# A gated feed-forward kernel on one core: its last store is made by two queues, half of the partitions each

## The chip, the cores and the metric

The kernel runs on one core of a Trainium2 chip. The metric is device time in microseconds: how long one execution takes. The core has a matrix engine (TensorE, PE in the profile), VectorE (DVE), ScalarE (ACT), GpSimd (POOL) and SyncE (SP). Transfers between device memory and the core's memory are started by an engine's queue and carried by 16 DMA engines.

## The reference

```python
B, S, D, F = 32, 32, 1024, 3584        # x: (B, S, D); w_gate, w_up: (D, F); w_down: (F, D); all bf16
def reference(x, w_gate, w_up, w_down):
    return (_gelu(x @ w_gate) * (x @ w_up)) @ w_down      # _gelu: the tanh approximation
```

With the batch flattened, x has N = 1024 rows. The result is 1024 x 1024 in bf16.

## The kernel before

There are two phases of matmuls. In the first, chunks of 128 columns of F (28 of them) are multiplied for 256 or 512 rows of x at a time: eight matmuls for the gate and eight for the up product, ScalarE applies the gelu (line 444), and VectorE multiplies the two and leaves the product in `hT` (line 484). In the second phase (lines 411 to 428) the output is made in jobs: a job is one block of 128 rows (`tc`) and a stretch of columns, and takes 28 matmuls that add up in one bank of PSUM. Sixteen jobs of 512 columns would cover the output; the last of them is cut into one of 384 and one of 128 columns, so there are NJ = 17. The last job, number 16, is the one of 128 columns.

Every engine runs its own program, and waits on counters (semaphores). The program of each engine is written as a function: `prog_sp`, `prog_act`, `prog_pool`, `prog_pe`, `prog_dve`. A `_Clock` is one semaphore with the count that it will have reached; `do` issues an instruction and adds to a clock, and `wait` (line 41 emits it) holds an engine until a clock has reached a value. DMA clocks go up by 16 for each transfer.

The results of jobs leave PSUM in turns: even jobs by ScalarE (line 450), odd jobs by VectorE (line 490), both into `osb`, which is the same memory as `xT` and appears under that name in the profile. After each eviction SyncE stores the job's columns to the output, one DMA for a job, all on SyncE's own queue and on the clock `Q_OUT` (line 343). After the last one it waits for `Q_OUT` to reach its total, and with that the kernel ends. So the last steps in order are: last matmul of job 16 on TensorE, eviction of 128 x 128 by ScalarE, store of 128 partitions x 256 bytes (32 KB) by SyncE, and SyncE's wait for its landing.

ScalarE also has a DMA queue, which it uses for a part of x at the start (lines 296 and 287); it issues no transfer after that.

Of the kernel before, what the change touches and what calls it, by code (L numbers as in the profile page):

```python
# [5 lines left out]
P = 128  # L6
# [78 lines left out]
def bass_standalone__geglu_ffn__sampling_kernel(  # L85
# [120 lines left out]
    jobs.append((ltc, lcol + lnc - P, P, 0 if lbank != 0 else 2))  # L206
    NJ = len(jobs)

    def evac_eng_is_act(ji):
        return ji % 2 == 0  # L210

    out_r = of.rearrange("(tc p) d -> p tc d", p=P)
# [7 lines left out]
    C_ACT = _Clock("act")  # L220
# [7 lines left out]
    Q_WD_SP = _Clock("wd_sp", 16)  # L228
    Q_WD_POOL = _Clock("wd_pool", 16)
    Q_OUT = _Clock("out", 16)  # L230
    all_clocks = [C_PE, C_ACT, C_DVE, C_POOL, *Q_XA, *Q_X.values(), *Q_W0.values(), *Q_WG, *Q_WU,
                  Q_WD_SP, Q_WD_POOL, Q_OUT]

    ctx = _Ctx()

    with ExitStack() as es:
# [18 lines left out]
        osb = xT  # L255
# [14 lines left out]
        def issue_wd(ew, eng, mine, upto_chunk, clock, force=False):  # L270
            for k in list(mine):
                if force or wd_gate_chunk[k] <= upto_chunk:
                    ew.wait(C_PE, ctx.get(("U", last_part[wd_gate_chunk[k]])))
                    a, b = wd_groups[k]
                    ew.do(lambda: eng.dma_start(wd[:, a:b, :], wd_r[:, a:b, :]), clock=clock)  # L275
                    mine.remove(k)

        def load_w(ew, eng, w, j):
            c0, gsz, buf = groups[j]
            q = (Q_WG if w == "wg" else Q_WU)[j]  # L280
            ctx.set((w, j), ew.do(lambda: eng.dma_start(  # L281
                wbuf(w, buf)[:, :, 0:gsz * P], w_r[w][:, :, c0 * P:(c0 + gsz) * P]), clock=q))
# [12 lines left out]
        def early_loads(ew, eng, side):  # L295
            ctx.set(("xa", side), ew.do(lambda: eng.dma_start(  # L296
                xa[:, side, :], xa_r[:, side, :]), clock=Q_XA[side]))
            yield
            if side == 0:
                for k in range(DK):  # L300
                    for w in ("wg", "wu"):
                        load_w0(ew, eng, w, k)
            ew.wait(Q_W0[("wu", 5)], ctx.get(("wu0", 5)))
            for q in XPIECES:
                load_x(ew, eng, q, side)

        def gate_w(ew, j):
            if war[j] is None:
                for s in range(2):
                    ew.wait(Q_X[(XC2, s)], ctx.get(("x", XC2, s)))  # L310
                return -1
            ew.wait(C_PE, ctx.get(("U", last_part[war[j]])))
            return war[j]
# [15 lines left out]
        def prog_sp(eng):  # L329
            sp = _Eng(ctx, eng, None)  # L330
            for _ in early_loads(sp, eng, 0):
                pass
            wd_mine = [k for k in range(len(wd_groups)) if k % 2 == 0]
            for j in range(NG):
                known_chunk = gate_w(sp, j)
                load_w(sp, eng, "wg", j)
                issue_wd(sp, eng, wd_mine, known_chunk, Q_WD_SP)
            issue_wd(sp, eng, wd_mine, FM, Q_WD_SP, force=True)
            ctx.set("wd_sp_total", Q_WD_SP.n)
            last = None  # L340
            for ji, (tc, col0, ncols, b) in enumerate(jobs):
                sp.wait(C_ACT if evac_eng_is_act(ji) else C_DVE, ctx.get(("E", ji)))
                last = sp.do(lambda: eng.dma_start(
                    out_r[:, tc, col0:col0 + ncols],
                    osb[:, tc, col0:col0 + ncols]), clock=Q_OUT)
            sp.wait(Q_OUT, last)

        def turn_xa(pe, eng, b, dk):
            pe.wait(Q_XA[b], ctx.get(("xa", b)))
            j, (bank, k0, k1, b0, b1) = next(  # L350
                (j, c) for j, c in enumerate(XA_PS) if c[1] <= dk < c[2] and c[3] <= b < c[4])
            o = P * ((b1 - b0) * (dk - k0) + b - b0)
            last = dk == k1 - 1 and b == b1 - 1
            v = pe.do(lambda: eng.matmul(  # L354
                ps[:, bank, o:o + P],
                xa[:, b, :].rearrange("p (j k) -> p j k", k=DK)[:, :, dk],
                ident[:, :], start=(dk == k0 and b == b0), stop=last), mark=last)
            if last:
                ctx.set(("XP", j), v)
# [36 lines left out]
        def prog_pe(eng):  # L396
# [14 lines left out]
            for ji, (tc, col0, ncols, b) in enumerate(jobs):  # L411
                if b in bank_last_job:
                    pj = bank_last_job[b]
                    pe.wait(C_ACT if evac_eng_is_act(pj) else C_DVE, ctx.get(("E", pj)))
                else:
                    pe.wait(C_DVE, ctx.get(("D", owner[b])))
                bank_last_job[b] = ji
                v = None
                for m in range(FM):
                    pe.wait(C_DVE, ctx.get(("D", last_part[m])))  # L420
                    last = (m == FM - 1)
                    v = pe.do(lambda: eng.matmul(  # L422
                        ps[:, b, 0:ncols],
                        hT[:, m, tc * P:(tc + 1) * P],
                        wd[:, m, col0:col0 + ncols],
                        start=(m == 0), stop=(m == FM - 1),
                    ), mark=last)
                ctx.set(("O", ji), v)

        def prog_act(eng):  # L430
            act = _Eng(ctx, eng, C_ACT)
            act.do(lambda: eng.activation(warm[:, 0:1], const0, ACTF.Gelu_apprx_tanh))
            for _ in early_loads(act, eng, 1):
                for j, (bank, k0, k1, b0, b1) in enumerate(XA_PS):
                    act.wait(C_PE, ctx.get(("XP", j)))
                    nt = P * (b1 - b0)
                    ctx.set(("XA", j), act.do(lambda: eng.activation(  # L437
                        xT[:, k0:k1, P * b0:P * b1],
                        ps[:, bank, 0:nt * (k1 - k0)].rearrange("p (k t) -> p k t", t=nt), ACTF.Copy)))
            for i, (m, t0, t1, (gb, g0, g1), us) in enumerate(parts):  # L440
                act.wait(C_PE, ctx.get(("U" if us[0] == gb else "G", i)))
                if i >= NTB:
                    act.wait(C_DVE, ctx.get(("D", i - NTB)))
                ctx.set(("A", i), act.do(lambda: eng.activation(  # L444
                    t_bufs[i % NTB][:, 0:t1 - t0], ps[:, gb, g0:g1], ACTF.Gelu_apprx_tanh)))
            for ji, (tc, col0, ncols, b) in enumerate(jobs):
                if not evac_eng_is_act(ji):
                    continue
                act.wait(C_PE, ctx.get(("O", ji)))
                ctx.set(("E", ji), act.do(lambda: eng.activation(  # L450
                    osb[:, tc, col0:col0 + ncols], ps[:, b, 0:ncols], ACTF.Copy)))

        def prog_dve(eng):
            dve = _Eng(ctx, eng, C_DVE)
# [37 lines left out]

        progs = [
            (prog_sp, nc.sync, "sync"),
            (prog_act, nc.scalar, "scalar"),
            (prog_pool, nc.gpsimd, "gpsimd"),
            (prog_pe, nc.tensor, "tensor"),
# [44 lines left out]
```

## Time and profile before

| what | us |
|---|---|
| median of 3 runs | 299.48 (299.15 to 299.63) |
| the profiled execution, its time | 298.94 |
| the profiled execution, its span | 297.6 |
| TensorE busy in the span | 293.6 |
| VectorE, ScalarE, GpSimd busy | 64.3, 42.4, 7.9 |
| last eviction by ScalarE: start, length | 295.85, 0.28 |
| last store's issue by SyncE: start, length | 296.15, 0.33 |
| last store, from issue to landing | 1.4 |
| SyncE's last wait, for that landing | 1.1 |

The span is what the profile sees of the program; the execution's time holds a little more than it. All times inside the profile count from the span's start. SPq, ACTq and PEq are the queues of instructions of SyncE, ScalarE and TensorE, and DMA_DIRECT2D is the instruction that issues a transfer; its length is the time of the issue alone, and the bytes move afterwards. Times of landing count from the issue.

### The profile page before, as it was taken

The numbers are of one execution on the slowest core, as the hardware profiler recorded it, in microseconds if no ns is written. First come the engines' busy times: TensorE is split into PE (matmuls) and PEld (weight loads), VectorE is DVE, ScalarE is ACT, GpSimd is POOL, SyncE is SP. The second block draws the span as 40 slices with busy tenths as digits, with TensorE's granted clock in tenths as the row PEclk, the third lists the DMA queues.
The fourth block names the chain that finished last, engine by engine and source line by source line (L and its number), as shares of the span: only waits on it lengthen the run. The fifth ranks groups of instructions, "written<-read, shape, count | busy, mean of one in ns | idle before, by whom it ended". The sixth has DMA issues, their size and how long they took to land.

```text
span 297.6 us, 3491 instructions
## 1 busy us (share of the span) xinstructions
PE 293.6 (99%) x1528; PEld 147.9 (50%) x1552; DVE 64.3 (22%) x108; ACT 42.4 (14%) x79; POOL 7.9 (3%) x14
## 2 busy tenths in 40 slices
PE   8999999999999999999999999999999999999997
PEld 5899644444444444444444444444444444444445
DVE  4669721111121111122111122110000000000000
ACT  4032211221111121111121111110000000000000
POOL 1001001020000002001000000000000000000000
DMA  7988004766009301942104000000000100010001
GB/s 263 391 194 263 23 2 147 276 203 224 0 0 305 120 0 38 373 156 100 43 0 141 0 2 0 0 0 20 18 18 20 35 18 18 20 35 18 18 20 35
DMA packets 17806, 26.43 MB, mean 89 GB/s; under 512 B 1152, under 2 KB 11392, under 8 KB 17792
## 3 DMA queue, kind: packets, MB, share of 16 engines
q1 hardware_dynamic: 13840, 16.78, 17.2%
q0 software_dynamic: 2176, 8.39, 7.8%
q10 hardware_dynamic: 1776, 1.05, 1.4%
q8 instruction: 12, 0.20, 0.3%
q14 instruction: 2, 0.02, 0.0%
HBM read 24.12 MB, written 2.10 MB: 88 GB/s over the span
## 4 chain that ended last, share of the span: by engine, by line
PE 97%; DMA 1%; issue 0%; SPq 0%; ACT 0%
PE ps L385 65%; PE ps L422 32%; DMA wgbig<-in_w_gate_dram 1%; SPq L296 0%; ACT xT L450 0%
## 5 line engine op out<-in xcount | busy, mean ns | idle before, releaser
L422 PE MATMUL ps<-wd,hT 128*128 128x512 bf16 (+2 forms) x468 | 96.5, 366 | 0.4
L385 PE MATMUL ps<-xT,wubig 128*128 128x512 bf16 (+2 forms) x395 | 79.5, 336 | 0.3
L385 PE MATMUL ps<-xT,wgbig 128*128 128x512 bf16 (+2 forms) x394 | 79.2, 336 | 0.4
L422 PEld LDWEIGHTS ps<-wd,hT 128*128 128x128 bf16 x476 | 45.5, 98 | 51.6
L484 DVE TENSOR_TENSOR hT<-tb,ps 128x512 bf16<-128x512 f32 (+1 forms) x64 | 38.9, 613 | 131.6 <-PE ps L385 131.6
L444 ACT ACTIVATE tb<-ps 128x512 f32<-128x512 f32 (+1 forms) x64 | 34.3, 544 | 158.0 <-PE ps L385 157.5
L385 PEld LDWEIGHTS ps<-xT,wgbig 128*128 128x128 bf16 x400 | 38.1, 98 | 31.8 <-DVE xT L475 0.3
L385 PEld LDWEIGHTS ps<-xT,wubig 128*128 128x128 bf16 x400 | 38.1, 98 | 31.5 <-DMA wubig<-in_w_up_dram 0.2
L385 PE MATMUL ps<-xT,wgsmall 128*128 128x512 bf16 x126 | 30.1, 379 | 0.1
L385 PE MATMUL ps<-xT,wusmall 128*128 128x512 bf16 x125 | 29.8, 379 | 0.2
L490 DVE CAST xT<-ps 128x512 bf16<-128x512 f32 (+1 forms) x8 | 5.4, 675 | 89.6 <-PE ps L422 89.6
L385 PEld LDWEIGHTS ps<-xT,wgsmall 128*128 128x128 bf16 x128 | 12.5, 98 | 15.1
L385 PEld LDWEIGHTS ps<-xT,wusmall 128*128 128x128 bf16 x128 | 12.5, 98 | 15.1
L450 ACT ACTIVATE xT<-ps 128x512 bf16<-128x512 f32 (+1 forms) x9 | 5.1, 562 | 93.1 <-PE ps L422 93.1
L475 DVE STREAM_TRANSPOSE xT<-hT 128x128 bf16<-128x128 bf16 (+2 forms) x20 | 13.5, 708 | 4.7 <-DMA hT<-in_x_dram 4.7
L460 DVE STREAM_TRANSPOSE xT<-hT 32x192 bf16<-32x192 bf16 x16 | 8.2, 515 | 4.6 <-DMA hT<-in_x_dram 4.2
L281 POOL DMA_DIRECT2D wubig<-in_w_up_dram x3 | 2.7, 886 | 63.1 <-PE ps L385 63.1
L399 PE MATMUL ps<-const-bfloat16-1.0 128*128 128x512 bf16 (+1 forms) x10 | 3.0, 476 | 0.8 <-PEq L527 0.8
L281 POOL DMA_DIRECT2D wusmall<-in_w_up_dram x2 | 2.0, 994 | 47.1 <-PE ps L385 26.0
L275 POOL DMA_DIRECT2D wd<-in_w_down_dram x3 | 2.3, 768 | 19.1 <-PE ps L385 19.1
L399 PEld LDWEIGHTS ps<-const-bfloat16-1.0 128*128 128x128 bf16 x10 | 1.2, 134 | 2.4 <-issue 2.4
L437 ACT ACTIVATE xT<-ps 128x128 bf16<-128x128 f32 (+1 forms) x4 | 1.5, 437 | 1.9 <-PE ps L354 1.9
(10 smaller groups left out, 4.5 us busy)
## 6 DMA issues: line engine op xcount, KB each, us to landing
wd<-in_w_down_dram SPq DMA_DIRECT2D x4, 1024.0 KB, 11.4
wgbig<-in_w_gate_dram SPq DMA_DIRECT2D x3, 1024.0 KB, 5.7
wubig<-in_w_up_dram POOLq DMA_DIRECT2D x3, 1024.0 KB, 9.7
wd<-in_w_down_dram POOLq DMA_DIRECT2D x3, 1024.0 KB, 11.4
wgbig<-in_w_gate_dram SPq DMA_DIRECT2D x8, 256.0 KB, 5.4
wubig<-in_w_up_dram SPq DMA_DIRECT2D x8, 256.0 KB, 5.5
wgsmall<-in_w_gate_dram SPq DMA_DIRECT2D x2, 1024.0 KB, 5.9
wusmall<-in_w_up_dram POOLq DMA_DIRECT2D x2, 1024.0 KB, 9.6
```

What stands on the lines that cost most here:

```text
L275: ew.do(lambda: eng.dma_start(wd[:, a:b, :], wd_r[:, a:b, :]), clock=clock)
L281: ctx.set((w, j), ew.do(lambda: eng.dma_start(wbuf(w, buf)[:, :, 0:gsz * P], w_r[w][:, :, c0 * P:(c0 + gsz) * P]), clock=q))
L385: v = pe.do(lambda: eng.matmul(ps[:, bank, f0:f1], wbuf(w, buf)[:, dk, slot * P:(slot + 1) * P], xT[:, dk, t0:t1], start=first, stop=last ...
L399: pe.do(lambda: eng.matmul(ps[:, 0, 0:n], ones_w, ones_x[:, 0:n], start=True, stop=True), mark=False)
L422: v = pe.do(lambda: eng.matmul(ps[:, b, 0:ncols], hT[:, m, tc * P:(tc + 1) * P], wd[:, m, col0:col0 + ncols], start=(m == 0), stop=(m == F ...
L437: ctx.set(("XA", j), act.do(lambda: eng.activation(xT[:, k0:k1, P * b0:P * b1], ps[:, bank, 0:nt * (k1 - k0)].rearrange("p (k t) -> p k t" ...
L444: ctx.set(("A", i), act.do(lambda: eng.activation(t_bufs[i % NTB][:, 0:t1 - t0], ps[:, gb, g0:g1], ACTF.Gelu_apprx_tanh)))
L450: ctx.set(("E", ji), act.do(lambda: eng.activation(osb[:, tc, col0:col0 + ncols], ps[:, b, 0:ncols], ACTF.Copy)))
L460: v = dve.do(lambda: eng.transpose(xT[32 * a:32 * (a + 1), XA_DVE[0]:XA_DVE[1], XA[0]:XA[1]].rearrange("p k (b t) -> p k b t", t=P)[:, :, ...
L475: v = dve.do(lambda: eng.transpose(xT[:, dk, q[0]:q[1]].rearrange("p (c i) -> p c i", i=32), src))
L484: ctx.set(("D", i), dve.do(lambda: eng.tensor_tensor(hT[:, m, t0:t1], t_bufs[i % NTB][:, 0:t1 - t0], ps[:, ub, u0:u1], ALU.mult)))
L490: ctx.set(("E", ji), dve.do(lambda: eng.tensor_copy(osb[:, tc, col0:col0 + ncols], ps[:, b, 0:ncols])))
```

## The change

The last store, of job 16, is split by partitions. SyncE stores partitions 0 to 63 on `Q_OUT`, and ScalarE stores partitions 64 to 127 on its own queue and a new semaphore, `Q_OUT2`, after it has waited for its own eviction to be counted. SyncE at the end waits for both semaphores. The other 16 stores stay as they were. The new assertion states that the last job is one that ScalarE evicts.

```diff
+    assert NJ % 2 == 1
+
     def evac_eng_is_act(ji):
         return ji % 2 == 0
...
     Q_OUT = _Clock("out", 16)
+    Q_OUT2 = _Clock("out2", 16)
...
             for ji, (tc, col0, ncols, b) in enumerate(jobs):
                 sp.wait(C_ACT if evac_eng_is_act(ji) else C_DVE, ctx.get(("E", ji)))
+                p1 = P // 2 if ji == NJ - 1 else P
                 last = sp.do(lambda: eng.dma_start(
-                    out_r[:, tc, col0:col0 + ncols],
-                    osb[:, tc, col0:col0 + ncols]), clock=Q_OUT)
+                    out_r[0:p1, tc, col0:col0 + ncols],
+                    osb[0:p1, tc, col0:col0 + ncols]), clock=Q_OUT)
             sp.wait(Q_OUT, last)
+            sp.wait(Q_OUT2, ctx.get("out2"))
...
                 ctx.set(("E", ji), act.do(lambda: eng.activation(
                     osb[:, tc, col0:col0 + ncols], ps[:, b, 0:ncols], ACTF.Copy)))
+            act.wait(C_ACT, ctx.get(("E", NJ - 1)))
+            ctx.set("out2", act.do(lambda: eng.dma_start(
+                out_r[P // 2:P, tc, col0:col0 + ncols],
+                osb[P // 2:P, tc, col0:col0 + ncols]), clock=Q_OUT2))
```

More of the change, by code (lines that the diff above doesn't have):

```diff
@@ L230, in bass_standalone__geglu_ffn__sampling_kernel @@
     Q_OUT = _Clock("out", 16)
+    Q_OUT2 = _Clock("out2", 16)
     all_clocks = [C_PE, C_ACT, C_DVE, C_POOL, *Q_XA, *Q_X.values(), *Q_W0.values(), *Q_WG, *Q_WU,
-                  Q_WD_SP, Q_WD_POOL, Q_OUT]
+                  Q_WD_SP, Q_WD_POOL, Q_OUT, Q_OUT2]
     ctx = _Ctx()
```

## The prediction

> **What bounds the kernel now.** I read the engine table, then the chain of waits, then the last microseconds as a timeline, in windows and by transfers, because the edit touches only the last store.
>
> The engine table and the summary of the chain:
>
> ```profile
> PE 293.6 (99%) x1528; PEld 147.9 (50%) x1552; DVE 64.3 (22%) x108; ACT 42.4 (14%) x79; POOL 7.9 (3%) x14
> ...
> PE 97%; DMA 1%; issue 0%; SPq 0%; ACT 0%
> ```
>
> TensorE is never short of work, and 97% of the chain is matmuls. Nothing that the edit changes lies in them. The chain written out in time ends like this (start, length, what):
>
> ```profile
> 281.55 14.28 PE ps L422 x93
> 295.82 0.02 issue
> 295.85 0.28 ACT xT L450
> ```
>
> After the last matmul ScalarE evicts the last 128 columns from 295.85 to 296.13. The timeline shows what follows (start, length, engine; SPq is SyncE's queue):
>
> ```profile
> 295.85 0.28 ACT L450 ACTIVATE xT<-ps 128x128 bf16<-128x128 f32 x1 [5.52 <-PE ps L422]
> 296.15 0.33 SPq L343 DMA_DIRECT2D out_dram<-xT  x1
> ```
>
> and three windows split the rest (window, length, busy time of five engines, clock, share of the DMA engines, GB/s):
>
> ```profile
> 296.15:296.95 0.80, 0.00 (x0) 0.00 (x0) 0.00 (x0) 0.00 (x0) 0.00 (x0) 1.00 0.00 0
> 296.95:297.25 0.30, 0.00 (x0) 0.00 (x0) 0.00 (x0) 0.00 (x0) 0.00 (x0) 1.00 0.50 109
> 297.25:297.62 0.37, 0.00 (x0) 0.00 (x0) 0.00 (x0) 0.00 (x0) 0.00 (x0) 1.00 0.00 0
> ```
>
> The tail is thus 1.47 us: 0.80 until the first byte moves (0.33 of it the issue), 0.30 of moving, 0.37 until SyncE sees the completion and stops. No compute engine works in it. Only this tail, 0.5% of the span, is open to the change.
>
> **The reference point.** The profiled execution took 298.94 us: span 297.6 and 1.3 outside it. The median of the runs is 299.48 (299.15 to 299.63), so the profiled one is 0.5 lower. The sum below is a difference in the profiled tail, and I add it to the median. About 0.2%, or 0.6 us, is what a measurement of this kernel can tell from no change; "same" means within that.
>
> **SyncE's half.** It waits for the same eviction and issues at 296.15 as before. The store goes from 128 rows of 256 bytes to 64. Two prices are open. The issue: stores of 128, 96 and 32 KB all took 0.33, so it does not follow bytes, and a load with only 32 partitions (the x pieces, line 287) took 0.33 too, so it does not seem to follow partitions either, though that one still had 128 pieces in all. I take 0.33; if it halved it would give 0.16. The rest, from the list of transfers (size, median us from issue to landing):
>
> ```profile
> out_dram<-xT SPq DMA_DIRECT2D x15, 128.0 KB, 1.7
> ...
> out_dram<-xT SPq DMA_DIRECT2D x1, 96.0 KB, 1.6
> out_dram<-xT SPq DMA_DIRECT2D x1, 32.0 KB, 1.4
> ```
>
> 96 KB less saves 0.3 us, so 16 KB less saves 0.05; if the moving phase halved with the rows it would save 0.15. But the other 16 KB move at the same moment, so the 32 KB of before still have to pass. I take 0 and keep 0.05 and 0.15 as lower bounds, 0.31 with the halved issue.
>
> A rule speaks against the change here. The Trainium skill, in "DMA: Bandwidth & Descriptors", section "Rules for kernel authors", says of two transfers to disjoint partition halves that they share the same 16 DMA engines and serialize, and advises one transfer of 128 partitions. By that rule the saving is the 0 that I took; by halving it would be 0.15. No run here shows the case.
>
> **ScalarE's half.** It is new, and nothing is queued behind it on ScalarE. It is the new end of the chain if it lands after SyncE's. Terms, each relative to SyncE's issue at 296.15:
> - It first waits for ScalarE's own eviction to be counted. The trace has no such wait on ScalarE. The nearest row is SyncE's start 0.02 after the eviction's end, which gives a lateness of 0. GpSimd's wait on its own iota (ends 1.06, next starts 1.15) is 0.09 long, so 0.07 late. GpSimd is a far relative; I take 0.03.
> - Issue on ScalarE is longer. In the pair of x loads at the start SyncE's took 0.38 and ScalarE's 0.40; in the pair at 12.61 they took 0.33 and 0.37. Also, ScalarE has issued nothing since about 16 us. SyncE's first store after an idle stretch of 48 us took 0.37, later ones 0.33. So between 0.02 and 0.08; I take 0.05.
> - ScalarE's queue may start late; that is the first rival below. In the sum it is 0.
>
> **SyncE's second wait.** SyncE now waits for two semaphores in turn. One such wait takes 0.02 (17 ns, SyncE's waits at line 41). The first passes while the second half is still on its way, so it is hidden if ScalarE's half is last, and costs 0.02 if not. I take 0.02.
>
> **The rest.** The list of instructions of the new kernel shows one more DMA on ScalarE, 64x128, after the last eviction, and SyncE's last store cut to 64x128; every other engine has the same list. PE, DVE and GpSimd do nothing in the tail. So: 0 + 0.03 + 0.05 + 0.02 = +0.10 us, that is 299.48 + 0.10 = 299.58, a hair slower and not measurable.
>
> **Rival 1, slower: ScalarE's queue lags.** The only place where both queues start together on quiet DMA engines is the load of x at the start:
>
> ```profile
> 0.73 0.38 SPq L296 DMA_DIRECT2D hT<-in_x_dram  x1
> ...
> 0.79 0.40 ACTq L296 DMA_DIRECT2D hT<-in_x_dram  x1
> ```
>
> ```profile
> hT<-in_x_dram SPq DMA_DIRECT2D x1, 256.0 KB, 2.8
> hT<-in_x_dram ACTq DMA_DIRECT2D x1, 256.0 KB, 3.3
> ```
>
> Counted from its own issue, ScalarE's landed 0.5 later. If that lag belongs to the queue, the end moves by 0.5 and the upper ends of the other terms, 0.07 + 0.08 + 0.02: +0.67, giving 300.15, slower by 0.22%. Against it: those transfers are 256 KB each, which at the 393 GB/s of the window from 2.70 to 3.70 need 0.65 to move, so the second may only have stood behind the first's bytes; 16 KB at 109 GB/s take 0.15. And among the smaller x pieces (64 KB) the medians are 3.8 and 3.9, a lag of 0.1. The rival decides once the lag passes 0.5. Chance 0.20.
>
> **Rival 2, a little slower: one issue at a time.** If ScalarE's issue can't begin before SyncE's 0.33 is over, the end moves by 0.33 + 0.10 = +0.43: 299.91, still within 0.2%. The pair at 12.61 speaks against it: both issues began at 12.61 and took 0.33 and 0.37, so neither stood still for the other's 0.33. Chance 0.10. The Trainium skill has such a rule in "Perfetto Trace Analysis", section "DMA Instruction — HWDGE (DVE, Sync)": the descriptor generator is locked for the exclusive use of one sequencer, and the wait for it lies inside the profiled duration. The trace does not agree, at least at the size of 0.33, in that pair.
>
> **Rival 3, faster: the halves run truly beside each other.** Then both the moving phase and the issue shrink with the rows: 0.15 + 0.16 = 0.31 less, 299.17. To be measurably faster it would have to take 0.6 out of a tail of 1.47, of which 0.37 is completion after the last byte and 0.47 (0.80 less 0.33) passes between the end of the issue and the first byte; together with the issue these fixed parts are nearly all of the 1.4 to which the landing fell from 1.7 when the bytes fell to a quarter. Chance 0.12.
>
> That the change doesn't do what it says can be left out: the two stores of 64 rows stand on the two engines in the list of instructions.
>
> **How the numbers follow.** Forecast 0.58 at 299.58; rival 1 0.20 at 300.15; rival 2 0.10 at 299.91; rival 3 0.12 at 299.17. The runs of before spread by 0.3 downward and 0.15 upward of their median, so a case near a border falls on both sides. Slower by over 0.2% (above 300.08): 0.17 from rival 1, 0.04 from rival 2, 0.03 from the forecast: 0.24. Faster by over 0.2% (below 298.88): 0.07 from rival 3, which also stands for any shrinking of the fixed parts that no row shows, and 0.02 from the forecast: 0.09. The rest, 0.67, is within. The range goes from 299.15, where rival 3 lies, to 300.15, where rival 1 does.
>
> **What would show it.** In the changed kernel's profile ScalarE's store should start at 296.15 to 296.22 on the scale of this span and last 0.35 to 0.41; SyncE's should start 0.02 after the eviction's end and last 0.33; both should land 1.35 to 1.5 after their issue; and SyncE's last wait should be for ScalarE's semaphore. A lag of 0.5 or more between the two landings makes rival 1 right, an issue of 0.65 or more on one of the two makes rival 2 right, and landings of 1.2 or less with a shorter issue make rival 3 right. If the time moves by over 0.6 us while the tail moves by less than 0.3, the cause lies in something that I held to be untouched, and the prediction is wrong in its premise.

## The result, and the profile after

The change makes the kernel slower: 300.10 us median against 299.39 (14 runs each), ratio 1.0024 with a 95% interval of 1.0017 to 1.0032. At 299.39 that is 0.51 to 0.96 us, 0.72 in the middle. The middle lies just beyond the 0.2% that the prediction set as the border of what can be told, the lower end just short of it.

TensorE is again busy for 99% of the span, and the chain (the work that ended last, followed back) is again matmuls; the chain of before began with a load, 1% of it, which the edit does not touch. The 2.0 us more of TensorE are no sign of more work: the profile of before holds only 1528 of the 1552 matmuls.

```profile
PE 295.6 (99%) x1552; PEld 148.6 (50%) x1552; DVE 64.4 (22%) x108; ACT 42.3 (14%) x79; POOL 7.9 (3%) x14
...
PE 99%; ACT 0%; issue 0%
```

This execution's span is 298.8, 1.2 more than the one of before, and half of that has nothing to do with the edit: the last eviction starts at 296.45 instead of 295.85, before any changed instruction runs. Such starts scatter from one profiled execution to the next (296.06 to 297.11 in the experiments), so below only the tail is compared, from the issue of the last store to the end of the span. The timeline of the tail (start, length, engine):

```profile
296.45 0.28 ACT L455 ACTIVATE xT<-ps 128x128 bf16<-128x128 f32 x1 [5.52 <-PE ps L427]
296.75 0.55 SPq L347 DMA_DIRECT2D out_dram<-xT  x1
296.75 0.56 ACTq L458 DMA_DIRECT2D out_dram<-xT  x1
```

Both queues start in the same moment, 0.02 after the eviction, but the issues take 0.55 and 0.56 where SyncE's took 0.33 before. The windows of the tail (window, length, busy time of five engines, clock, share of the DMA engines, GB/s):

```profile
296.75:297.95 1.20, 0.00 (x0) 0.00 (x0) 0.00 (x0) 0.00 (x0) 0.00 (x0) 1.00 0.00 0
297.95:298.20 0.25, 0.00 (x0) 0.00 (x0) 0.00 (x0) 0.00 (x0) 0.00 (x0) 1.00 0.32 66
298.20:298.45 0.25, 0.00 (x0) 0.00 (x0) 0.00 (x0) 0.00 (x0) 0.00 (x0) 1.00 0.33 66
298.45:298.84 0.39, 0.00 (x0) 0.00 (x0) 0.00 (x0) 0.00 (x0) 0.00 (x0) 1.00 0.00 0
```

Nothing moves for 1.20 us (0.80 before). Then there are two moving phases of 0.25, one after the other: by the packets' records the first holds only packets of SyncE's queue, the second only those of ScalarE's. The completion takes 0.39 (0.37 before). The tail is 2.09 against 1.47: +0.62, which lies inside the interval of the timed runs. The transfers (size, us from issue to landing):

```profile
out_dram<-xT SPq DMA_DIRECT2D x1, 16.0 KB, 1.8
out_dram<-xT ACTq DMA_DIRECT2D x1, 16.0 KB, 2.0
```

Half of the bytes take 1.8 to land on the queue that took 1.4 for all of them, and SyncE's last wait lasts 1.5 instead of 1.1.

### The profile page after: what moved, and what is told of

Read it like the earlier page. It is cut to its first block, busy times and chain, and to the rows that moved or that the text cites. A ratio compares the mean times of both kernels' runs of the same rounds, so it can differ in the third digit from the quotient of the medians.

```text
span 298.8 us, 3516 instructions
## 1 busy us (share of the span) xinstructions
PE 295.6 (99%) x1552; PEld 148.6 (50%) x1552; DVE 64.4 (22%) x108; ACT 42.3 (14%) x79; POOL 7.9 (3%) x14
## 4 chain that ended last, share of the span: by engine, by line
PE 99%; ACT 0%; issue 0%
PE ps L390 65%; PE ps L427 32%; PE ps L404 1%; PE ps L359 0%; ACT xT L455 0%
## 5 line engine op out<-in xcount | busy, mean ns | idle before, releaser
L390 PE MATMUL ps<-xT,wgbig 128*128 128x512 bf16 (+2 forms) x400 | 80.5, 339 | 0.0
```

Source lines behind the costliest of these rows:

```text
L390: v = pe.do(lambda: eng.matmul(ps[:, bank, f0:f1], wbuf(w, buf)[:, dk, slot * P:(slot + 1) * P], xT[:, dk, t0:t1], start=first, stop=last ...
```

## The experiments

Three theories were to be told apart: A, two issues in the same moment stretch each other; B, a store of 64 rows is itself slow; C, ScalarE's queue is slow. The tails of all timed kernels, from the records of the trace in us, stand in one table. Each row is one profiled execution; the ratio is of the timed runs. "First byte" counts from the start of the store's own issue, in the order of the issues.

| kernel | issue | first byte | tail | tail less 1.47 | ratio to before (95%) |
|---|---|---|---|---|---|
| before | 0.33 | 0.83 | 1.47 | | |
| the change | 0.55, 0.56 | 1.21, 1.47 | 2.09 | +0.62 | 1.0024 (1.0017 to 1.0032) |
| both halves on SyncE | 0.55, then 0.60 | 1.21, 1.25 | 2.46 | +0.99 | 1.0032 (1.002 to 1.0044) |
| whole on ScalarE | 0.37 | 0.87 | 1.53 | +0.05 | 1.0002 (0.9992 to 1.0012) |
| SyncE's half alone | 0.55 | 1.21 | 1.80 | +0.33 | 1.0009 (0.9997 to 1.0022) |
| ScalarE's half later | 0.55, 0.53 | 1.21, 1.19 | 2.15 | +0.68 | 1.0024 (1.0013 to 1.0035) |
| halves by columns | 0.33, 0.37 | 0.83, 0.91 | 1.64 | +0.17 | 1.0008 (0.9994 to 1.0021) |
| 96 and 32 rows | 0.35, 0.38 | 0.85, 0.93 | 1.68 | +0.20 | 1.0005 (0.9996 to 1.0014) |
| the change, not for the first time | 0.47, 0.51 | 1.13, 1.39 | 2.02 | +0.54 | 1.0012 (0.9998 to 1.0026) |

**Both halves on SyncE.** The second queue is taken away, the cut by partitions stays.

```diff
+            ctx.set("out2", sp.do(lambda: eng.dma_start(
+                out_r[P // 2:P, tc, col0:col0 + ncols],
+                osb[P // 2:P, tc, col0:col0 + ncols]), clock=Q_OUT2))
...
-            act.wait(C_ACT, ctx.get(("E", NJ - 1)))
-            ctx.set("out2", act.do(lambda: eng.dma_start(
...
```

> SyncE issues both halves, one after the other, on its own queue; ScalarE issues none. Theory A (two issues at once stretch each other): no two issues overlap, so each takes 0.33 as before, the first half lands 1.4 after its issue, the second is issued about 0.4 later and lands 1.4 to 1.5 after that: end 0.35 to 0.45 later than before, 0.2 to 0.3 earlier than the change. Theory B (a store of 64 rows is itself slow to issue): both issues take 0.55, the second half lands about 0.6 + 1.8 after the first issue: end 0.8 to 1.0 later than before, later than the change. Theory C (ScalarE's queue is slow): as A, the end 0.35 to 0.45 later than before.

Timeline of its two issues:

```profile
296.37 0.55 SPq L347 DMA_DIRECT2D out_dram<-xT  x1
296.96 0.60 SPq L350 DMA_DIRECT2D out_dram<-xT  x1
```

The first takes 0.55 with no other issue beside it, and the end is 0.99 later. Theory A falls, B holds. The second issue's 0.60 says less: in the probes below, stores of other counts took as long when they came right behind a store of 64 rows. So the second queue saves something against one queue (2.09 against 2.46); the cut itself is what loses.

**Whole on ScalarE.** The cut is taken away, the other queue stays.

```diff
+                if ji == NJ - 1:
+                    continue
...
-                out_r[P // 2:P, tc, col0:col0 + ncols],
...
+                out_r[0:P, tc, col0:col0 + ncols],
...
```

> ScalarE alone issues the last store, whole, 128 rows; SyncE only waits for it. Theory A: no second issue beside it, so ScalarE's issue takes 0.35 to 0.41, landing 1.4 to 1.55, end 0.0 to 0.15 later than before. Theory B: the store has 128 rows, so the same as A. Theory C: issue 0.55 and landing 2.0, end 0.55 to 0.7 later than before, all that the change cost.

```profile
297.42 0.37 ACTq L459 DMA_DIRECT2D out_dram<-xT  x1
```

The issue takes 0.37, the landing 1.5, and the time is that of before. Theory C falls: ScalarE's queue, unused for 280 us, costs about 0.05.

**SyncE's half alone.** Partitions 64 to 127 of the last job are left unstored, and ScalarE issues nothing.

> SyncE stores partitions 0 to 63 of the last job as in the change; partitions 64 to 127 of the last job are not stored at all, and ScalarE issues nothing. Theory A: nothing overlaps, so the issue takes 0.33 or less, landing 1.3 to 1.4, end 0 to 0.15 earlier than before. Theory B: issue 0.55, landing 1.8, end about 0.3 to 0.4 later than before. Theory C: as A.

```profile
296.53 0.55 SPq L347 DMA_DIRECT2D out_dram<-xT  x1
```

Theory B again: with half of the store thrown away and nothing beside it, the issue takes 0.55, the first byte comes at 1.21 and the tail grows by 0.33. The ratio alone (its interval includes 1) would not have shown it; the tail does.

**ScalarE's half later.** ScalarE makes two scratch evictions before it issues.

```diff
-            act.wait(C_ACT, ctx.get(("E", NJ - 1)))
+            for k in range(2):
+                v = act.do(lambda: eng.activation(t_bufs[k][:, 0:P], ps[:, b, 0:P], ACTF.Copy))
+            act.wait(C_ACT, v)
```

> As the change, but ScalarE makes two more evictions of the same 128 columns into scratch (about 0.28 each) before it issues its half, so that its issue begins about 0.6 after SyncE's. Theory A: SyncE's issue is over by then and takes 0.33 again, its half lands 1.4 after the issue; ScalarE's issue takes 0.35 to 0.41 and lands 1.4 to 1.5 after it: end 0.6 to 0.7 later than before, about equal to the change although ScalarE started 0.6 later. Theory B: both issues take 0.55 as in the change, end 1.1 to 1.2 later than before. Theory C: SyncE's issue 0.33, ScalarE's 0.55 and landing 2.0: end 1.1 to 1.2 later.

The two evictions overlapped each other and the one before, so that ScalarE issued 0.34 after SyncE and not 0.6; the expected ends do not apply as written. Still, both issues keep their 0.53 to 0.55 although ScalarE's starts when SyncE's is more than half over. ScalarE's first byte comes 1.19 after its issue instead of 1.47, so that 0.34 of delay at the issue cost only 0.06 at the end. Counted from its own issue, ScalarE's half lands after 1.76 here and after 2.04 in the change, where its first byte comes 0.27 after SyncE's.

**Which counts of rows are slow.** Two probes cut the stores of jobs 1 to 14 (6 us apart) in many ways on SyncE's queue; the edit only changes which rows and columns each store takes, and sends the rest right after the first part of the next job's store. The issues compared here are those of the first parts, which have nothing directly in front of them in the queue.

> A probe of store shapes on SyncE's queue alone. The stores of jobs 1 to 14, about 6 us apart and long landed before the end, are cut: the first part goes out after its eviction, the rest right after the first part of the next job's store. First parts: 64, 96, 32, 16, 112, 64 (the upper ones), 80 and 48 rows of 512 columns; 64 rows of two separate stretches of 128 columns; 128 rows of two such stretches; 32 rows of four stretches of 64; 128 rows of 128 and of 64 columns; 64 rows of 128. The last store is whole, as before. What is asked is the length of each issue. Theory B1 (fewer than 128 rows cost 0.2 us of issue): 0.55 for every first part with fewer than 128 rows, whatever its columns and pieces, 0.33 for 128 rows. Theory B2 (fewer than 128 pieces cost it): 64 rows of two stretches and 32 rows of four are 128 pieces and take 0.33; 64, 96, 32, 16 rows of one stretch take more than 0.33. Theory B3 (only the count of 64 is slow): 0.55 for 64 rows alone, 0.33 for the other counts. Theory A (two at once) says 0.33 throughout, and has lost already for SyncE.

Issues of 64 rows, 32 rows, 64 rows of two separate stretches of columns, 32 rows of four stretches, and 64 rows of 128 columns, in that order, from the timeline of the first probe:

```profile
212.52 0.54 SPq L339 DMA_DIRECT2D out_dram<-xT  x1
224.61 0.32 SPq L339 DMA_DIRECT2D out_dram<-xT  x1
248.78 0.63 SPq L339 DMA_DIRECT2D out_dram<-xT  x1
260.87 0.33 SPq L339 DMA_DIRECT2D out_dram<-xT  x1
278.90 0.47 SPq L339 DMA_DIRECT2D out_dram<-xT  x1
```

16, 48, 80 and 112 rows took 0.32 to 0.34, 96 rows and 128 rows of 128 columns 0.36, the upper 64 rows 0.47. Only the count of 64 is slow (theory B3): not fewer rows, not fewer pieces (64 rows of two stretches are 128 pieces and take 0.63; 32 rows of four are as many and take 0.33), not the bytes. It is slow with 128 and with 512 columns, and dearer at its first use than later.

The rest of each job shows one thing more. A store of a quick count took 0.32 to 0.47 to issue when it was sent right behind another quick one, and 0.58 to 0.61 right behind one of 64 rows, even with 16, 32, 120 or 128 rows. This is the store of 16 rows behind the upper 64:

```profile
243.16 0.58 SPq L339 DMA_DIRECT2D out_dram<-xT  x1
```

> A second probe of store shapes on SyncE's queue, made like the first: the first parts of the stores of jobs 1 to 14 are 32 rows of two separate stretches (64 pieces), 64 rows from the middle (32 to 95), 64, 63, 65, 56, 72, 8 rows, 64 rows of four stretches, 60 rows, 96 rows of two stretches, 64 rows, 120 rows, 32 rows. If the count of 64 rows alone is slow: 0.47 to 0.55 for each part of 64 rows wherever it lies, more with more stretches, and below 0.40 for all others, 32 rows of two stretches too. If 64 pieces are what is slow, 32 rows of two stretches take 0.47 or more. Odd counts (63, 65) or counts that 16 does not divide may spread over fewer DMA engines and take another time; nothing in the case says which.

From the second probe: 32 rows of two stretches, 63 rows, and 65:

```profile
212.38 0.34 SPq L339 DMA_DIRECT2D out_dram<-xT  x1
230.41 0.33 SPq L339 DMA_DIRECT2D out_dram<-xT  x1
236.56 0.31 SPq L339 DMA_DIRECT2D out_dram<-xT  x1
```

64 rows from the middle took 0.62 and 64 rows of four stretches 0.65; 8, 56, 60, 72, 96 (two stretches) and 120 rows took 0.28 to 0.34. The two neighbours of 64 are quick to issue. The store of 63 rows then met something else: 56 of its rows had moved 1.3 us after the issue, but the last seven moved only from 232.13 on, when a 16 KB transfer on the queue of instructions, begun at 230.74, was over; and the store sent right behind it took 1.75 to issue, which no other did. Why 64 is slow, no run shows.

**Pairs.** A probe sends parts of the even jobs from SyncE and ScalarE in the same moment.

> A probe of pairs. At even jobs, about 12 us apart, SyncE and ScalarE each store a part in the same moment, after ScalarE's eviction: 64 + 64 rows of 512 columns; 128 rows, 256 + 256 columns; 128 rows, 64 + 64 columns; 64 + 64 rows of 128 columns (the change's own shape); ScalarE alone a whole 128 x 512; SyncE alone 64 rows; ScalarE alone 64 rows; 64 + 64 rows of two stretches of 128 columns. What is left over goes out later on SyncE; the last store is whole on SyncE, as before. If two issues in the same moment hinder each other only in what comes after the issue: 0.55 on both for pairs of 64 rows, 0.33 and 0.37 for pairs of 128 rows, ScalarE's half landing 0.2 to 0.3 later than SyncE's in each pair, and ScalarE alone landing 1.75 after its issue with 64 rows. If they stretch each other's issue: 0.55 or more on the pairs of 128 rows as well. If ScalarE's queue is slow by itself: its 64 rows alone land 2.0 after the issue.

A pair of 64 + 64 rows, and one of 128 rows cut by columns:

```profile
207.45 0.55 SPq L342 DMA_DIRECT2D out_dram<-xT  x1
207.45 0.56 ACTq L342 DMA_DIRECT2D out_dram<-xT  x1
...
219.53 0.36 SPq L342 DMA_DIRECT2D out_dram<-xT  x1
219.54 0.38 ACTq L342 DMA_DIRECT2D out_dram<-xT  x1
```

ScalarE alone took 0.47 for 64 rows, which landed after 1.93 (SyncE's alone after 1.92), and 0.34 for a whole store: the price of 64 belongs to both queues, and a pair of 128 rows pays nothing of it. ScalarE's first byte was 0.28 behind SyncE's in the first pair, 0.09 in the second, and 0.09 in a later pair of exactly the change's shape (the fourth, with issues of 0.51 and 0.50). The lag is not simply a wait until SyncE's bytes are through: in the first pair they move for 0.45, and ScalarE's begin 0.17 before they end.

**Halves by columns.** The two queues stay, each with 128 rows of 64 columns.

```diff
-                p1 = P // 2 if ji == NJ - 1 else P
+                n1 = ncols // 2 if ji == NJ - 1 else ncols
...
-                out_r[P // 2:P, tc, col0:col0 + ncols],
...
+                out_r[:, tc, col0 + ncols // 2:col0 + ncols],
...
```

> The last store is split between the two queues as in the change, but by columns: SyncE stores 128 rows of the first 64 columns, ScalarE 128 rows of the other 64. If the rows are what cost (theory B): both issues 0.33 to 0.37, first bytes 0.80 after them, ScalarE's half behind SyncE's by 0.1 to 0.3, tail from the end of the eviction 1.6 to 1.8 us: end 0.1 to 0.3 later than before and 0.3 to 0.5 earlier than the change. If two issues at once stretch each other: both 0.55, tail 2.1, as the change.

```profile
296.36 0.33 SPq L347 DMA_DIRECT2D out_dram<-xT  x1
296.37 0.37 ACTq L458 DMA_DIRECT2D out_dram<-xT  x1
```

The same cut in two without the count of 64: issues of before, ScalarE's first byte 0.08 behind SyncE's, tail +0.17. That is what a second queue costs here when the rows are right, and it still gains nothing.

**96 and 32 rows.** One number of the change is altered, `p1 = 96`, with ScalarE's rows from 96 on.

> As the change, but SyncE stores 96 rows of the last job and ScalarE the other 32. If the count of 64 is what cost (theory B3): issues 0.32 to 0.37 on both, first bytes 0.82 to 0.95 after them, tail from the end of the eviction 1.55 to 1.70 us against 1.50 before and 2.12 in the change: end 0.05 to 0.2 later than before, 0.4 to 0.55 earlier than the change. If any split by rows over two queues costs it: 0.55 on both, tail about 2.1.

```profile
296.86 0.35 SPq L347 DMA_DIRECT2D out_dram<-xT  x1
296.86 0.38 ACTq L458 DMA_DIRECT2D out_dram<-xT  x1
```

A cut by partitions without a 64 costs 0.20 instead of 0.62. SyncE's part lands after 1.47 instead of 1.79, which is the price of the count. ScalarE's first byte is 0.09 behind instead of 0.27, and that is not the count's doing alone, as the next run shows.

**Not for the first time.** Earlier stores are made as pairs too, the last one as in the change.

> The change's last store, with four earlier stores (jobs 0, 2, 4, 6) also made as pairs of 64 rows on the two queues, job 8 with 96 rows on ScalarE, and jobs 10, 12 and 14 as pairs of 96 and 32 rows; all of these land long before the end. If a part of the price belongs to the first use of a 64-row store: the first pair takes about 0.55 on both with ScalarE's first byte 0.28 behind SyncE's, the later pairs about 0.50 with 0.1 behind, and the last store's tail is 1.85 to 1.95 instead of 2.12: end 0.35 to 0.45 later than before. If each use costs the same: 0.55 and a tail of 2.1 at the end. Pairs of 96 and 32 rows: 0.32 to 0.38 on both.

```profile
296.53 0.47 SPq L342 DMA_DIRECT2D out_dram<-xT  x1
```

The issue falls from 0.55 to 0.47, as in the probe (ScalarE's from 0.56 to 0.51), and the tail by 0.08 to 2.02, less than the 0.17 to 0.27 expected: ScalarE's first byte stayed 0.27 behind SyncE's. So the lag does not belong to the first use. In the second of its pairs ScalarE's bytes went first and SyncE's came 0.28 behind. Nor does it belong to 64 rows: in the three earlier pairs of 96 and 32 rows of 512 columns, whose issues took 0.32 to 0.38, ScalarE's first byte was 0.35 behind.

No run beat the kernel before. A whole store of 128 rows of 64 columns landed 1.44 after its issue in the first probe, one of 128 columns 1.47: even half of the bytes would win 0.03.

## Why the prediction was right and wrong

- **Where the change acts: right.** The tail went from 1.47 to 2.09; no other stage that the edit touches moved. The sum of the likeliest case (+0.10) was wrong. The end lay where rival 1 was put (300.15 against 300.10 measured), but only half by its mechanism, so that it fell inside the range is in part luck. "Slower by over 0.2%" had been given 0.24, "within" 0.67; and counted from the prediction's own 299.48, the ratio would give 300.20, just outside.
- **SyncE's half: the step that failed.** The term was 0, from "it does not seem to follow partitions either", read off the load with 32 partitions and bounded by a halving of the issue. Measured alone, it is +0.33: issue 0.55, first byte at 1.21. The row was not near enough: among stores, 32 is a quick count and 64 a slow one. The bounds reached below zero (0.31 less) and not above it, and the price lay above.
- **The moving phase: right that nothing is saved, wrong that both halves move at the same moment.** Two phases of 0.25 follow each other where one of 0.30 was. The Trainium skill's rule in "DMA: Bandwidth & Descriptors", section "Rules for kernel authors", that transfers to disjoint partition halves serialize, agrees with these two windows. Other pairs overlap in part: the probe's first by 0.17, and the columns' pair, whose first bytes are 0.08 apart.
- **ScalarE's wait for its own eviction: too dear.** 0.03 was taken, the trace shows 0: both issues start within 4 ns of each other. GpSimd was a poor relative.
- **ScalarE's longer issue: right for a store of 128 rows.** 0.05 was taken; the whole store on ScalarE cost 0.05. For 64 rows it is 0.56, the same as SyncE's.
- **SyncE's second wait: 0.02 taken, 0.01 measured.** The last wait's instruction takes 28 ns instead of 17.
- **Rival 1: a real term, half its size, put at 0 in the sum.** ScalarE's landing is 0.26 behind SyncE's, not 0.5 or more, and its first byte 0.27. The prediction's counter-argument, that a lag is a wait for the bytes in front, fits the change, where SyncE's phase of 0.25 comes first, but not the probe's first pair, which overlaps and lags as much. It is no fixed property of ScalarE's queue either: the fourth pair lags by 0.09, and in one pair SyncE's bytes came second. What sets it stays open.
- **Rival 2: no.** By its own mark (0.65 or more on one issue) it did not occur. Issues in the same moment with 128 rows of 64 columns take 0.33 and 0.37; a whole store alone takes 0.33 on SyncE and 0.34 to 0.37 on ScalarE. The Trainium skill's "Perfetto Trace Analysis", section "DMA Instruction — HWDGE (DVE, Sync)", has a lock with a wait inside the profiled length; these issues leave room for 0.04 of it at most, not for 0.33.
- **Rival 3: no.** It let the issue shrink with the rows, and the issue grew from 0.33 to 0.55.

Put together: +0.33 for a 64-row store on SyncE (about 0.08 of it for the first use), and +0.29 more because ScalarE's half comes behind it, 0.62 in all. Two things are left open: why 64 is slow, and why the second queue's first byte lags by 0.27 to 0.36 in some pairs and by less than 0.10 in others.

## What to carry to other kernels

A store of a few tens of KB at the end of a kernel is almost all fixed cost (here the bytes move for 0.30 of 1.47 us), so cutting it in two multiplies what is fixed and shares what is small; keep it whole on one idle queue. Price a transfer by a row of the same shape, and where the trace has none, put one into a hidden place of the kernel and read its issue, because a count of rows can cost more than the bytes. When a change moves the time by a few tenths of a us, compare the tail in the trace: it showed +0.33 where the timed ratio could not tell.

## What the runs showed of the hardware

With nothing directly in front of it in its queue, a store of exactly 64 partitions took 0.47 to 0.51 us to issue (0.53 to 0.56 at the first use, 0.62 to 0.67 where the rows came from the middle (one store) or were in several stretches), on SyncE's queue as on ScalarE's, and SyncE's first byte came 1.12 to 1.30 us after the start of the issue (1.42 in the pair where ScalarE's went first). Stores of 8, 16, 32, 48, 56, 60, 63, 65, 72, 80, 96, 112, 120 and 128 rows took 0.28 to 0.38, and on one queue alone their first byte came after 0.75 to 0.87; for the first two-stretch store of 128 rows it was 0.39 and 0.91. Right behind a 64-row store in the same queue, the issue of other counts took 0.58 to 0.61. Where both queues stored in the same moment, the second first byte came 0.08 to 0.10 or 0.27 to 0.36 after the first. Loads of 64 rows were not tried.
